# Two linear steps of the VectorE exponential moved to GpSimd, in an attention and MLP block

## Chip, cores, metric

One core of a Trainium2 chip runs the whole program. The metric is the time of one execution on the device, in microseconds (us). Engine names in the profile: PE is TensorE (PEld its weight loads), DVE is VectorE, ACT is ScalarE, POOL is GpSimd, SP is SyncE. The granted clock is the share of TensorE's full clock that the profiler records as granted. PSUM holds the results of TensorE's matmuls; the tiles named `..._sb` lie in SBUF, the on-chip working memory.

A run: "slow" can only mean that it lay more than 1.5% above the fastest run of the same kernel.

## The reference, cut to what matters

```python
def _A_ref(x, wqkv, wo):                      # S = 2048, D = 640, 32 heads of 20
    qkv = (x @ wqkv).reshape(B, S, 3, H, Dh)...
    scores = einsum("bhqd,bhkd->bhqk", q, k) * Dh ** -0.5
    p = softmax(scores)                        # 32 x 2048 x 2048 exponentials
    o = einsum("bhqk,bhkd->bhqd", p, v)
    return o... @ wo
def _B_ref(x, w1, b1, w2, b2):                 # token-mixing MLP, 2048 -> 1536 -> 2048
    ...
xn = layernorm(x)
return x + _A_ref(xn, ...) * silu(_B_ref(xn, ...))
```

The exponentials dominate: 2048 blocks of 128 keys by 512 queries, called units below.

## The kernel before

The program is laid out when it is built. A list scheduler gives every instruction a cost in ns, keeps a clock for each engine, and always places the candidate that can start first. The result is a fixed order for each engine; on the chip an engine runs its order from front to back, and waits on semaphores where data or buffers need it.

```python
def _add(self, eng, ceng, fn, reads, writes, name, extra_req=(), cost=100.0, tail=None):
    ...
    start = self.T[eng]                        # the planner's clock of this engine
    for tt in req.values():                    # what it reads or overwrites
        start = max(start, tt.fin + (self.LAT[eng] if tt.ceng != eng else 0.0))
    ...
    self.T[eng] = start + cost
    t.fin = start + cost + (self.TAIL[eng] if tail is None else tail)
```

ScalarE takes two units in one instruction, from two groups of two PSUM banks. VectorE takes one unit at a time from each of two more banks (4 and 5), by a polynomial on the bits of the score:

```python
ACT_GROUPS = ((0, 1), (2, 3))
DVE_GROUPS = ((4,), (5,))
...
ch = [   # one chain; k is the bank's index
    (lambda e: e.tensor_scalar(w3, lo, 0x7FFF, None, ALU.bitwise_and), bs, [sw], dv(N)),          # PSUM
    (lambda e: e.tensor_scalar(v_, w_, 1.0 / 256.0, -128.0, ALU.mult, ALU.add), [sw], [sv], dv(N, .26)),
    (lambda e: e.tensor_scalar(l_, w_, a3 / 65536.0, (b3 - 64.0 * a3) / 256.0, ALU.mult, ALU.add),
     [sw], [sl_], dv(N, .26)),
    (lambda e: e.tensor_tensor(l_, v_, l_, ALU.mult), [sv, sl_], [sl_], dv(N, .52)),               # product
    (lambda e: e.tensor_tensor(l_, l_, w_, ALU.mult), [sl_, sw], [sl_], dv(N, .52)),               # product
    (lambda e: e.scalar_tensor_tensor(o_, zr, -(self.OFFS - 16256.0), l_, ALU.add, ALU.add),       # PSUM
     bs + [sl_], [S_(f"dpt{s0 + i}") for i in range(n)], dv(N)),
]
```

How many units VectorE gets is decided while the order is laid out: at each refill of a ScalarE group, every VectorE bank that is free by the planner's clock gets a unit in the same batch of score matmuls.

```python
def do_st(grp, us):
    ...
    for dg in self.DVE_GROUPS:
        if dgrp_state[dg] == "free" and len(lst) + len(dg) <= 4 ... and pr.ready("pe", [], [bank_slot[b] for b in dg]) <= T:
            lst += take_dve(dg, rows)
            banks += list(dg)
    emit_st(lst, banks)
```

TensorE's other work (projections, the MLP, products with V) is placed between these batches, along with filler matmuls that the planner adds wherever it counts too few columns in a window, to hold TensorE's granted clock.

The softmax here doesn't subtract the row's maximum and nothing guards it: scores larger than these inputs give would overflow.

Of the kernel before, what the change touches and what calls it, by code (L numbers as in the profile page):

```python
# [7 lines left out]
ALU = mybir.AluOpType  # L8
# [274 lines left out]
class _Kern:  # L283
# [25 lines left out]
    DVE_TAIL_GUARD = 3  # L309
    LAST_GUARD = 10  # L310
    NTMP = 4
    WARM = True
    WARM_MIN = 180.0
    WARM_SLACK = 30.0
# [87 lines left out]
    def schedule(self):  # L402
        pr, t = self.prog, self.t
# [21 lines left out]
        def S_(name):  # L425
            s = sl.get(name)
            if s is None:
                s = sl[name] = _Slot(name)
            return s
# [12 lines left out]
        def dv(n, rate=1.04):  # L442
            return 75.0 + n * rate
# [51 lines left out]
        def small(fn):  # L495
            def f(e):
# [12 lines left out]
                name="id1", cost=300)  # L509
# [5 lines left out]
               cost=200)  # L515
# [8 lines left out]
               writes=[S_("pad")], name="pad", cost=150)  # L524
        pr.dve(lambda e: e.tensor_reduce(cst_sb[:, 1:2], onerow, mybir.AxisListType.X, ALU.add), reads=[S_("idf")],
               writes=[S_("row")], name="pad", cost=130)
        for col, a_, b_, src in ((3, -1.0, 1.0, 0), (4, -CQ0, CQ0, 0), (5, QC, 0.0, 1), (6, KC, 0.0, 1)):
            pr.dve(lambda e, col=col, a_=a_, b_=b_, src=src: e.tensor_scalar(
                cst_sb[:, col:col + 1], cst_sb[:, src:src + 1], a_, b_, ALU.mult, ALU.add),
                reads=[S_("pad"), S_("row")], writes=[S_("cq")], name="cq", cost=90)  # L530
# [535 lines left out]
        dexp = []  # L1066
# [79 lines left out]
        def can_exp():  # L1146
            if not pexp:
                return False
            n = len(pexp[0][0])
            s0 = ptr[0] if ptr[0] + n <= self.RP else 0  # L1150
            return not any(pt_busy[s0:s0 + n])

        dchains = []

        def start_dchain():

            us, banks, grp = dexp[0]
            n = len(us)
            if dptr[0] + n > self.DPT:
                dptr[0] = 0  # L1160
            s0 = dptr[0]
            dexp.pop(0)
            for i in range(n):
                dpt_busy[s0 + i] = True
            dptr[0] = (s0 + n) % self.DPT
            N = n * 512
            zr = ps_all[:, banks[0] * 512:banks[0] * 512 + N]
            lo = zr.bitcast(u16).rearrange("p (n two) -> p n two", two=2)[:, :, 0:1]
            k = self.DVE_GROUPS.index(grp)
            w_, v_, l_ = ew_sb[:, k, 0:N], ev_sb[:, k, 0:N], el_sb[:, k, 0:N]  # L1170
            sw, sv, sl_ = S_(f"ew{k}"), S_(f"ev{k}"), S_(f"el{k}")
            w3 = w_.rearrange("p (n one) -> p n one", one=1)
            o_ = dpt_sb[:, s0:s0 + n, :].rearrange("p a b -> p (a b)").bitcast(u16)
            bs = [bank_slot[b] for b in banks[:n]]
            a3, b3 = self.C3
            ch = [
                (lambda e: e.tensor_scalar(w3, lo, 0x7FFF, None, ALU.bitwise_and), bs, [sw], dv(N)),  # L1177
                (lambda e: e.tensor_scalar(v_, w_, 1.0 / 256.0, -128.0, ALU.mult, ALU.add), [sw], [sv], dv(N, .26)),  # L1178
                (lambda e: e.tensor_scalar(l_, w_, a3 / 65536.0, (b3 - 64.0 * a3) / 256.0, ALU.mult, ALU.add),  # L1179
                 [sw], [sl_], dv(N, .26)),  # L1180
                (lambda e: e.tensor_tensor(l_, v_, l_, ALU.mult), [sv, sl_], [sl_], dv(N, .52)),  # L1181
                (lambda e: e.tensor_tensor(l_, l_, w_, ALU.mult), [sl_, sw], [sl_], dv(N, .52)),  # L1182
                (lambda e: e.scalar_tensor_tensor(o_, zr, -(self.OFFS - 16256.0), l_, ALU.add, ALU.add),  # L1183
                 bs + [sl_], [S_(f"dpt{s0 + i}") for i in range(n)], dv(N)),
            ]
            dchains.append([(x, us, s0, grp) for x in ch])

        def emit_dchain(chn):
            (fn, rd, wr, cost), us, s0, grp = chn.pop(0)
            tk = pr.dve(fn, reads=rd, writes=wr, name=f"dexp{us[0]}", cost=cost)  # L1190
            if not chn:
                dchains.remove(chn)
                dgrp_state[grp] = "free"
                for i, u in enumerate(us):
                    avail.append((tk.fin, u, "d", s0 + i))
# [320 lines left out]
        def pe_cands(T):  # L1516
# [29 lines left out]
            if avail and acc_ok[0]:  # L1546
# [14 lines left out]
                if pick:  # L1561
                    r = max(x[0] for x in pick) + PV_MARGIN
                    pr_ = 1.0 if nav >= self.PV_HI else 30.0 if ramp[0] else (8.0 if pr.gate.warm or not self.WARM else 70.0)
                    c.append((pr_, max(r, pr.ready("pe", [], [sl_acc])), lambda pick=pick: emit_pv(pick)))
            if self.WARM:
                wb = warm_bank()
# [18 lines left out]
            for j in active:  # L1585
                s = j.steps[j.i]
                if s[0] == "pe":
                    c.append((j.prio if pr.gate.warm or not self.WARM else -2.0, pr.ready("pe", s[2], s[3]),
                              lambda j=j: do_step(j, "pe")))
# [60 lines left out]
        def do_step(j, eng):  # L1650
            s = j.steps[j.i]
            j.i += 1
            if s[0] == "ev":
                n = s[8]
                fn = ev_fn(s, eng)
                cost = ac(n) if eng == "act" else dv(n, 0.55 if s[7].startswith("xTe") else 1.04)
                getattr(pr, eng)(fn, reads=s[5], writes=s[6], name=s[7], cost=cost)
            elif s[0] == "pe":
                pe_full(s[1], s[2], s[3], s[4], s[5])
            else:  # L1660
                getattr(pr, s[0])(s[1], reads=s[2], writes=s[3], name=s[4], cost=s[5])
            settle(j)

        def eng_cands(eng, T):
            c = []
            for j in active:
                s = j.steps[j.i]
                if s[0] == eng:
                    c.append((j.prio, pr.ready(eng, s[2], s[3]), lambda j=j: do_step(j, eng)))
                elif s[0] == "ev" and (eng == "dve" or (eng == "act" and (ramp[0]))):  # L1670
                    pen = 0.0 if eng == "dve" else 0.0
                    c.append((j.prio - 30.0 + pen, pr.ready(eng, s[5], s[6]), lambda j=j: do_step(j, eng)))
            if eng == "act" and can_exp():
                us, banks, grp = pexp[0]
                c.append((30.0 if ramp[0] else 48.0, pr.ready("act", [bank_slot[b] for b in banks[:len(us)]], []), emit_exp))
            if eng == "dve":
                for chn in dchains:
                    (fn, rd, wr, cost) = chn[0][0]
                    c.append((90.0 - 0.1 * len(chn), pr.ready("dve", rd, wr), lambda chn=chn: emit_dchain(chn)))
                if dexp and not any(ch[0][3] == dexp[0][2] for ch in dchains):  # L1680
                    us, banks, grp = dexp[0]
                    n = len(us)
                    s0 = dptr[0] if dptr[0] + n <= self.DPT else 0
                    if not any(dpt_busy[s0:s0 + n]):
                        r = pr.ready("dve", [bank_slot[b] for b in banks[:n]], [])

                        def go():
                            start_dchain()
                            emit_dchain(dchains[-1])
                        c.append((90.0, r, go))  # L1690
            return c

        def warm_bank():
            if nxt[0] < 12:
                return AB
            if WB in busybanks or WB in bank_off:
                return None
            return WB
# [18 lines left out]
        while True:  # L1717
# [26 lines left out]
            for e in order:  # L1744
                cs = pe_cands(pr.T[e]) if e == "pe" else eng_cands(e, pr.T[e])
                cs_by[e] = cs

            bt = None
            for e in order:
                if not cs_by[e]:  # L1750
                    continue
                r = min(max(x[1], pr.T[e]) for x in cs_by[e])
# [4 lines left out]
            r, e = bt  # L1757
            if e == "dve" and nxt[0] >= NU:

                soon = [max(x[1], pr.T[e]) for x in cs_by[e] if x[0] <= 12.0]  # L1760
                if soon and min(soon) <= r + 130.0:
                    r = min(soon)
# [45 lines left out]
```

## Time and profile before

| | before |
|---|---|
| time | 869.83 us, median of 2 runs (867.17 to 872.49); 866.5 to 870.8 in the later sessions |
| busy: ScalarE, VectorE, TensorE, GpSimd | 98%, 95%, 92%, 2% |
| units on ScalarE, on VectorE | 1776 (888 instructions), 272 |
| TensorE's granted clock | 1.0 |

A page of the profile lists busy time by engine, then the chain of work that ended last (followed back from the last instruction to what released each step), then groups of equal instructions: count, busy us and mean ns, and the engine's idle time just before them with what ended it. The prediction shows the lines on which it rests.

### The profile page before, as it was taken

What the parts mean: (1) busy time and instruction counts of PE and PEld (TensorE: products, weight loads), DVE (VectorE), ACT (ScalarE), POOL (GpSimd) and SP (SyncE); (2) the same over time, 40 slices, a digit from 0 to 9 for tenths busy, and PEclk for the clock granted to TensorE, in tenths of its full rate; (3) what the DMA queues carried; (4) which work ended last, traced back from release to release, by engine and by line L of the source; (5) the groups of instructions that cost most, each with busy time, mean ns of one, the idle gap of its engine ahead of it and who ended that gap; (6) DMA issues with size and microseconds to landing.
All of it is one profiled execution on the core that took longest, in us unless ns stands there. A gap on an engine that the chain in (4) does not pass through costs nothing.

```text
span 864.8 us, 16498 instructions
## 1 busy us (share of the span) xinstructions
PE 798.6 (92%) x5828; PEld 257.1 (30%) x5918; DVE 823.5 (95%) x2047; ACT 845.3 (98%) x925; POOL 14.0 (2%) x23
## 2 busy tenths in 40 slices
PE   8899999999999999999999999999899998998997
PEld 5422222222222223222322222222222222232233
DVE  8889999999999999999999999999999999999996
ACT  7899999999999999999999999999999999999996
POOL 3200000000000000000000000000000000000000
PEclk9999999999999999999999999999999999999999
DMA  8241010011010313020013022123312201032121
GB/s 236 48 113 30 8 35 10 16 36 31 11 55 15 77 34 89 10 55 10 16 25 78 23 51 52 25 52 71 67 30 46 47 11 11 3 102 69 41 44 35
DMA packets 123350, 39.32 MB, mean 45 GB/s; under 512 B 84312, under 2 KB 122152, under 8 KB 123272
## 3 DMA queue, kind: packets, MB, share of 16 engines
q1 hardware_dynamic: 123272, 38.27, 19.3%
q8 instruction: 50, 0.82, 0.4%
q14 instruction: 28, 0.23, 0.1%
HBM read 25.88 MB, written 9.83 MB: 41 GB/s over the span
## 4 chain that ended last, share of the span: by engine, by line
ACT 87%; PE 10%; DVE 2%; issue 1%; ACTq 0%
ACT pt_sb L1137 85%; PE ps_all L1109 3%; PE ps_all L1224 1%; ACT zt_sb L843 1%; PE ps_all L755 1%; PE ps_all L1702 1%; PE ps_all L879 1%; ACT zt_sb L838 1%; DVE ew_sb L1177 0%; PE ps_all L683 0%; PE ps_all L1710 0%; PE ps_all L722 0%; PE ps_all L703 0%; DVE dpt_sb L1183 0%; DVE el_sb L1181 0%
## 5 line engine op out<-in xcount | busy, mean ns | idle before, releaser
L1137 ACT ACTIVATE pt_sb<-ps_all 128x1024 bf16<-128x1024 f32 x888 | 819.8, 1144 | 3.8 <-PE ps_all L1109 3.0
L1109 PE MATMUL ps_all<-qk_sb 32*128 32x512 bf16 (+1 forms) x2112 | 367.5, 377 | 48.7 <-ACT pt_sb L1137 37.0
L1177 DVE TENSOR_SCALAR ew_sb<-ps_all 128x512 uint16<-128x512 uint16 x272 | 184.2, 685 | 20.7 <-PE ps_all L1109 19.6
L1109 PEld LDWEIGHTS ps_all<-qk_sb 32*128 32x128 bf16 x2112 | 97.3, 91 | 347.2 <-ACT pt_sb L1137 300.7
L1183 DVE SCALAR_TENSOR_TENSOR dpt_sb<-ps_all,el_sb 128x512 uint16<-128x512 f32 x272 | 182.1, 684 | 1.8
L1224 PE MATMUL ps_all<-pt_sb,v_sb 128*32 128x512 bf16 (+1 forms) x1833 | 162.7, 378 | 0.3 <-issue 0.3
L1181 DVE TENSOR_TENSOR el_sb<-ev_sb,el_sb 128x512 bf16<-128x512 bf16 x272 | 111.1, 418 | 1.1
L1182 DVE TENSOR_TENSOR el_sb<-el_sb,ew_sb 128x512 bf16<-128x512 bf16 x272 | 110.3, 418 | 0.9
L1224 PE MATMUL ps_all<-dpt_sb,v_sb 128*32 128x512 bf16 (+1 forms) x279 | 83.7, 379 | 0.0
L810 PE MATMUL ps_all<-regB,regA 128*128 128x128 bf16 (+1 forms) x371 | 75.6, 300 | 2.9 <-issue 1.1
L1178 DVE TENSOR_SCALAR ev_sb<-ew_sb 128x512 bf16<-128x512 uint16 x272 | 75.3, 285 | 2.3
L810 PE MATMUL ps_all<-regC,regA 128*128 128x128 bf16 (+1 forms) x370 | 74.2, 300 | 1.8 <-issue 1.0
L1179 DVE TENSOR_SCALAR el_sb<-ew_sb 128x512 bf16<-128x512 uint16 x272 | 75.1, 284 | 0.0
L722 PE MATMUL ps_all<-xnT_sb,wqk_sb 128*112 128x512 bf16 x200 | 68.2, 405 | 0.4 <-DVE zt_sb L816 0.4
L1224 PEld LDWEIGHTS ps_all<-pt_sb,v_sb 128*32 128x32 bf16 x1833 | 35.4, 94 | 55.5 <-issue 50.4
L1702 PE MATMUL ps_all<-wrm_sb 128*128 128x512 bf16 (+1 forms) x117 | 35.2, 391 | 3.9 <-DVE ps_all L513 2.2
L810 PEld LDWEIGHTS ps_all<-regB,regA 128*128 128x128 bf16 x384 | 25.8, 97 | 39.1 <-issue 23.8
L810 PEld LDWEIGHTS ps_all<-regC,regA 128*128 128x128 bf16 x384 | 25.0, 97 | 39.8 <-issue 28.5
L1710 PE MATMUL ps_all<-wrm_sb,v_sb 128*128 128x512 bf16 x97 | 34.0, 385 | 1.3 <-issue 0.7
L755 PE MATMUL ps_all<-wv_sb,xnT_sb 128*128 128x160 bf16 (+1 forms) x160 | 33.8, 302 | 0.4 <-DVE pk_sb L1030 0.3
L879 PE MATMUL ps_all<-wo_sb,xnT_sb 128*128 128x128 bf16 (+3 forms) x152 | 30.4, 298 | 0.7 <-issue 0.5
L722 PEld LDWEIGHTS ps_all<-xnT_sb,wqk_sb 128*112 128x112 bf16 x200 | 20.7, 127 | 30.6 <-issue 13.4
(89 smaller groups left out, 354.9 us busy)
## 6 DMA issues: line engine op xcount, KB each, us to landing
regA<-in_B_w_dram SPq DMA_DIRECT2D x6, 1024.0 KB
regA<-in_B_w_dram SPq DMA_DIRECT2D x8, 768.0 KB
qkT_scratch_dram<-pk_sb SPq DMA_DIRECT2D x40, 112.0 KB
qk_sb<-qkT_scratch_dram SPq DMA_DIRECT2D x56, 80.0 KB
regA<-in_A_x_dram SPq DMA_DIRECT2D x6, 640.0 KB
on_scratch_dram<-on_sb SPq DMA_DIRECT2D x124, 20.0 KB
out_dram<-regC SPq DMA_DIRECT2D x3, 640.0 KB
wqk_sb<-in_A_wqkv_dram SPq DMA_DIRECT2D x2, 680.0 KB
```

The costliest lines, as they stand in the source:

```text
L722: steps.append(("pe", lambda e, dc=dc: e.matmul(ps_all[0:112, bk * 512:(bk + 1) * 512], wqk_sb[:, dc * 1280 + c0:dc * 1280 + c0 + 112], xn ...
L810: steps.append(("pe", lambda e, k=k: e.matmul(ps(bk, n), wap[:, k, col0:col0 + 128], rows[:, k, c0:c0 + n], start=(k == 0), stop=(k == nk ...
L1109: pr.pe(lambda e, outp=outp, lhsT=lhsT, rhs=rhs, g=g: e.matmul(outp, lhsT, rhs, start=True, stop=True, tile_position=(32 * g, 0)), reads=q ...
L1137: tk = pr.act(lambda e: e.activation(outp, inp, AF.Exp, bias=-self.OFFS * math.log(2.0) / 128.0, scale=math.log(2.0) / 128.0), reads=[bank ...
L1177: (lambda e: e.tensor_scalar(w3, lo, 0x7FFF, None, ALU.bitwise_and), bs, [sw], dv(N)),
L1178: (lambda e: e.tensor_scalar(v_, w_, 1.0 / 256.0, -128.0, ALU.mult, ALU.add), [sw], [sv], dv(N, .26)),
L1179: (lambda e: e.tensor_scalar(l_, w_, a3 / 65536.0, (b3 - 64.0 * a3) / 256.0, ALU.mult, ALU.add), [sw], [sl_], dv(N, .26)),
L1181: (lambda e: e.tensor_tensor(l_, v_, l_, ALU.mult), [sv, sl_], [sl_], dv(N, .52)),
L1182: (lambda e: e.tensor_tensor(l_, l_, w_, ALU.mult), [sl_, sw], [sl_], dv(N, .52)),
L1183: (lambda e: e.scalar_tensor_tensor(o_, zr, -(self.OFFS - 16256.0), l_, ALU.add, ALU.add), bs + [sl_], [S_(f"dpt{s0 + i}") for i in range( ...
L1224: pr.pe(lambda e, outp=outp, lhsT=lhsT, rhs=rhs, k=k, g=g: e.matmul(outp, lhsT, rhs, start=(k == 0), stop=(k == NB - 1), tile_position=(0, ...
L1702: pe_full(lambda e: e.matmul(ps(wb, n), wrm_sb[:, 0:P], wrm_sb[:, P:P + n], start=True, stop=True), [S_("warm"), S_("warm1")], [bank_slot[ ...
```

## The change

The intent is to use the idle GpSimd. VectorE is 95% busy, so two of its six steps, those with one SBUF input and a scalar multiply and add, go to GpSimd; VectorE should then have time for more units, and ScalarE fewer. The first and last steps, which read PSUM, stay on VectorE. The planner gets a cost of 560 ns for a GpSimd step.

```diff
+    POOL_TT = 1150.0
+    POOL_TS = 560.0
 ...
-    (lambda e: e.tensor_scalar(v_, w_, 1.0 / 256.0, -128.0, ALU.mult, ALU.add), [sw], [sv], dv(N, .26)),
+    (lambda e: e.tensor_scalar(v_, w_, 1.0 / 256.0, -128.0, ALU.mult, ALU.add), [sw], [sv], self.POOL_TS, "pool", True),
     (lambda e: e.tensor_scalar(l_, w_, a3 / 65536.0, (b3 - 64.0 * a3) / 256.0, ALU.mult, ALU.add),
-     [sw], [sl_], dv(N, .26)),
+     [sw], [sl_], self.POOL_TS, "pool", True),
 ... (the other four steps gain "dve" as their engine)
     def emit_dchain(chn):
-        (fn, rd, wr, cost), us, s0, grp = chn.pop(0)
-        tk = pr.dve(fn, reads=rd, writes=wr, name=f"dexp{us[0]}", cost=cost)
+        (fn, rd, wr, cost, eng, _), us, s0, grp = chn.pop(0)
+        tk = getattr(pr, eng)(fn, reads=rd, writes=wr, name=f"dexp{us[0]}", cost=cost)
 ... (the chain's next step is offered as a candidate to its own engine)
```

More of the change, by code (lines that the diff above doesn't have):

```diff
@@ L1176, in start_dchain @@
             ch = [
-                (lambda e: e.tensor_scalar(w3, lo, 0x7FFF, None, ALU.bitwise_and), bs, [sw], dv(N)),
-                (lambda e: e.tensor_scalar(v_, w_, 1.0 / 256.0, -128.0, ALU.mult, ALU.add), [sw], [sv], dv(N, .26)),
+                (lambda e: e.tensor_scalar(w3, lo, 0x7FFF, None, ALU.bitwise_and), bs, [sw], dv(N), "dve", False),
+                (lambda e: e.tensor_scalar(v_, w_, 1.0 / 256.0, -128.0, ALU.mult, ALU.add), [sw], [sv], self.POOL_TS, "pool", True),
                 (lambda e: e.tensor_scalar(l_, w_, a3 / 65536.0, (b3 - 64.0 * a3) / 256.0, ALU.mult, ALU.add),
-                 [sw], [sl_], dv(N, .26)),
-                (lambda e: e.tensor_tensor(l_, v_, l_, ALU.mult), [sv, sl_], [sl_], dv(N, .52)),
-                (lambda e: e.tensor_tensor(l_, l_, w_, ALU.mult), [sl_, sw], [sl_], dv(N, .52)),
+                 [sw], [sl_], self.POOL_TS, "pool", True),
+                (lambda e: e.tensor_tensor(l_, v_, l_, ALU.mult), [sv, sl_], [sl_], dv(N, .52), "dve", True),
+                (lambda e: e.tensor_tensor(l_, l_, w_, ALU.mult), [sl_, sw], [sl_], dv(N, .52), "dve", True),
                 (lambda e: e.scalar_tensor_tensor(o_, zr, -(self.OFFS - 16256.0), l_, ALU.add, ALU.add),
-                 bs + [sl_], [S_(f"dpt{s0 + i}") for i in range(n)], dv(N)),
+                 bs + [sl_], [S_(f"dpt{s0 + i}") for i in range(n)], dv(N), "dve", False),
             ]
@@ L1675, in eng_cands @@
                 c.append((30.0 if ramp[0] else 48.0, pr.ready("act", [bank_slot[b] for b in banks[:len(us)]], []), emit_exp))
+            if eng in ("dve", "pool"):
+                for chn in dchains:
+                    (fn, rd, wr, cost, en, _) = chn[0][0]
+                    if en == eng:
+                        r = pr.ready(eng, rd, wr)
+                        c.append((90.0 - 0.1 * len(chn), r, lambda chn=chn: emit_dchain(chn)))
             if eng == "dve":
-                for chn in dchains:
-                    (fn, rd, wr, cost) = chn[0][0]
-                    c.append((90.0 - 0.1 * len(chn), pr.ready("dve", rd, wr), lambda chn=chn: emit_dchain(chn)))
                 if dexp and not any(ch[0][3] == dexp[0][2] for ch in dchains):
```

## The prediction

> **What bounds the kernel now.** I read the page's busy shares first, then its chain that ended last, then the groups by line, then the waits, and last the timeline of two cycles of VectorE.
>
> From the page of the kernel before (busy us, share of the span, instructions; then the chain that ended last):
>
> ```profile
> PE 798.6 (92%) x5828; PEld 257.1 (30%) x5918; DVE 823.5 (95%) x2047; ACT 845.3 (98%) x925; POOL 14.0 (2%) x23
> ...
> ACT 87%; PE 10%; DVE 2%; issue 1%; ACTq 0%
> ```
>
> ScalarE is the bound: 98% busy, and 87% of the chain. VectorE (95%) and TensorE (92%) are close behind; GpSimd is empty. So the change takes work from an engine that is nearly full but is not itself the bound. A gain must come through ScalarE having less to do.
>
> From the groups of the same page (count, then busy us and mean ns of one, then idle before):
>
> ```profile
> L1137 ACT ACTIVATE pt_sb<-ps_all 128x1024 bf16<-128x1024 f32 x888 | 819.8, 1144 | 3.8 <-PE ps_all L1109 3.0
> ...
> L1177 DVE TENSOR_SCALAR ew_sb<-ps_all 128x512 uint16<-128x512 uint16 x272 | 184.2, 685 | 20.7 <-PE ps_all L1109 19.6
> ...
> L1183 DVE SCALAR_TENSOR_TENSOR dpt_sb<-ps_all,el_sb 128x512 uint16<-128x512 f32 x272 | 182.1, 684 | 1.8
> ...
> L1181 DVE TENSOR_TENSOR el_sb<-ev_sb,el_sb 128x512 bf16<-128x512 bf16 x272 | 111.1, 418 | 1.1
> L1182 DVE TENSOR_TENSOR el_sb<-el_sb,ew_sb 128x512 bf16<-128x512 bf16 x272 | 110.3, 418 | 0.9
> ...
> L1178 DVE TENSOR_SCALAR ev_sb<-ew_sb 128x512 bf16<-128x512 uint16 x272 | 75.3, 285 | 2.3
> ...
> L1179 DVE TENSOR_SCALAR el_sb<-ew_sb 128x512 bf16<-128x512 uint16 x272 | 75.1, 284 | 0.0
> ```
>
> A unit is one 128x512 block of exponentials. ScalarE takes two at a time: 888 x 2 = 1776; VectorE takes 272; the sum is 2048. The split is made when the kernel is built: a list scheduler with a cost for each instruction lays out each engine's order, and hands VectorE a unit whenever a VectorE bank is free at a ScalarE refill. The change alters that order everywhere, because two costs and an engine change.
>
> From the waits (total us, times, longest):
>
> ```profile
> PEld ps_all L1109 <- ACT pt_sb L1137: 300.7, 726, 0.9
> ```
>
> TensorE's score matmuls wait for ScalarE's banks. TensorE runs in order, so anything that holds one of its instructions delays ScalarE's next refill, and ScalarE has only two groups of banks, one cadence of cover.
>
> From the timeline of VectorE (start us, us, and count where equal neighbours are merged):
>
> ```profile
> 504.68 1.29 DVE L1177 TENSOR_SCALAR ew_sb<-ps_all 128x512 uint16<-128x512 uint16 x2 [0.41 <-PE ps_all L1109]
> 505.89 0.49 DVE L1178 TENSOR_SCALAR ev_sb<-ew_sb 128x512 bf16<-128x512 uint16 x2
> 506.29 0.49 DVE L1179 TENSOR_SCALAR el_sb<-ew_sb 128x512 bf16<-128x512 uint16 x2
> 506.70 0.42 DVE L1181 TENSOR_TENSOR el_sb<-ev_sb,el_sb 128x512 bf16<-128x512 bf16 x1
> 507.06 0.75 DVE L816 TENSOR_SCALAR zt_sb<-ps_all,b2h_sb 128x512 bf16<-128x512 f32 x1
> 507.73 0.41 DVE L1181 TENSOR_TENSOR el_sb<-ev_sb,el_sb 128x512 bf16<-128x512 bf16 x1
> 508.06 0.75 DVE L1182 TENSOR_TENSOR el_sb<-el_sb,ew_sb 128x512 bf16<-128x512 bf16 x2
> 508.74 1.28 DVE L1183 SCALAR_TENSOR_TENSOR dpt_sb<-ps_all,el_sb 128x512 uint16<-128x512 f32 x2
> 510.18 0.69 DVE L1177 TENSOR_SCALAR ew_sb<-ps_all 128x512 uint16<-128x512 uint16 x1 [0.16 <-PE ps_all L1109]
> ```
>
> Two things are to be seen. Rows overlap: the mean of 285 ns is a latency, and the next one starts 0.20 us later (505.89 to 506.29 for two). Start to start, a step costs 0.60 (PSUM), 0.20 (linear), 0.34 (product). And the two chains of VectorE, one for each of its banks, run almost **in step**: both first steps, both pairs of linear steps, both products, both last steps, with a cycle of 5.5 us.
>
> **What the Trainium skill says.** "SBUF — State Buffer", section "Who interferes with whom": GpSimd has no SBUF port pair of its own, it shares VectorE's second; a VectorE instruction with two SBUF inputs contends with a GpSimd instruction that reads SBUF, and the second to issue "fully blocks" until the first is done. The two products read two SBUF tensors each, so they are exposed; the two PSUM steps have at most one SBUF input and are not. No GpSimd work runs beside these products in the trace before, so it neither confirms nor denies this.
>
> "GPSIMD Engine Reference", section "4.1 Engine selection": one-input elementwise work there is "roughly line-rate". The trace has only memsets to compare: 128x640 at 632 ns and 128x1024 at 957 ns, so 0.85 ns an element and 90 ns fixed. An estimate from these rows for 512 elements is 0.52 us, near the 0.56 us the change assumes; GpSimd's 128x16 TENSOR_SCALAR, though, took 271 ns, so the latency may rather be 0.27 + 496 x 0.85 ns = 0.69 us.
>
> "Perfetto Trace Analysis", section "Optimizing Scalar/DVE Operations": moving work between VectorE and GpSimd "might not help", for the shared port. The trace before cannot test it.
>
> **The change part by part.**
> (1) Removed from VectorE: 2 x 0.20 = 0.40 us a unit, 272 x 0.40 = 109 us (the page's busy sums of 75.3 + 75.1 overstate it). A unit then costs 0.60 + 2 x 0.34 + 0.60 = 1.88 us against 2.28.
> (2) Added to GpSimd: two steps of 0.56 us, 1.12 us a unit; for some 290 units 325 us, under 40% of the span. Its total is no bound.
> (3) What ScalarE could gain: in the timeline 14 activations fill 13.13 us, so about 0.917 us for two units, 0.46 us a unit. VectorE's other work is 823.5 - 272 x 2.28 = 203 us. Were VectorE held only by its sum, it would take about 320 units at the same 95% ((0.95 x 845 - 203) / 1.88 = 319). ScalarE would shed 48 x 0.46 = 22 us: 848 us. That is the ceiling.
> (4) What the latency does to it. Both chains are in step, and both need GpSimd at the same moment. First steps at 0 and 0.6 us; the first chain's linear steps on GpSimd from about 0.8 to 1.95; the second's from 1.95 to 3.1; then its products and last step to about 4.7; then about 0.8 us until the bank is refilled and read. That is 5.5 us, no shorter than now: the 0.40 us gained on VectorE are paid back by 2 x 1.12 us in a row on GpSimd. Before, 136 pairs in about 805 us make a mean cycle of 5.92; if it becomes 5.6, 287 units fit, 15 more, and ScalarE sheds 15 x 0.46 = 7 us. From 870 that is 863 us with no contention.
> (5) Contention. In that picture the first chain's products are due at 2.1 us, just when GpSimd holds the port for the second chain's linear steps. Each meeting costs VectorE 0.3 us (half of one step) to 1.1 us (both steps); I take 0.6 us a cycle. The scheduler knows nothing of it, so the fixed order becomes wrong: VectorE's banks come free late, TensorE stands at the matmul meant for them, and ScalarE's refill stands behind it. Cover is about half a ScalarE cadence, 0.45 us on average, but does not always apply; I let 0.25 us a cycle through. 140 cycles x 0.25 = 35 us. 863 + 35 = 898, which I round to 895.
>
> **The rivals.**
> A: VectorE was holding back the split, the scheduler places the chains out of step, and the port matters little: the ceiling of (3), 846 to 855 us. For it: VectorE's 95%, and GpSimd idle. Against: chains fed by the same matmul batch and two steps in a row on GpSimd.
> B: balance. The longer chain eats the freed time, contention is hidden in VectorE's new slack (5% + 109/865 = 18%, less 3% for 15 more units of 1.88 us: 15%): 860 to 880 us. For it: the slack is real, and a GpSimd wait on a chain leaves VectorE other work.
> C: contention dominates, both linear steps block both products, or GpSimd takes 0.7 us or more with 16-bit integer input: 1 us a cycle let through is 140 us, some 960 us or more; the kernel also places filler matmuls, by its own model of time, to hold TensorE's granted clock (now in the top tenth in all slices), and a stretched order thins them out.
>
> **Range and chances.** My line lies between B and C. 895 us; 848 to 970 should hold it 8 times in 10: the low end is the ceiling, the high end some 0.8 us a cycle let through. Two per cent are 17 us, so faster means under 852: 0.13. Within: 0.30. Slower, above 887: 0.57.
>
> **What would show it.** The count of VectorE units: 285 to 300 for (4), near 320 for A. GpSimd's linear steps spaced 0.5 to 0.6 us for (2). For (5): mean time, or start to start, of the two products well above 418 ns and 0.34 us while the PSUM steps stay at 685 ns; new waits of VectorE for GpSimd; score matmuls waiting for VectorE's last step, now small; ScalarE's idle before its activations, now 3.8 us, grown by tens of us. I am wrong if the products keep their 418 ns, if ScalarE stays at 98%, or if the chains fall out of step.

## The result, and the profile after

The changed kernel took 945.75 us, median of 2 runs (943.54 to 947.96), against 869.83: a ratio of 1.0873 (95% interval 1.0693 to 1.1053). A ratio here and below is the mean time of one kernel's fast runs over that of the other's in the same rounds, so not quite the ratio of the medians quoted.

From the page of the changed kernel (shares, granted clock by slice in tenths, chain that ended last):

```profile
PE 876.1 (93%) x5915; PEld 266.5 (28%) x5915; DVE 785.8 (83%) x1539; ACT 862.3 (91%) x921; POOL 402.7 (43%) x585
...
PEclk9999999999999999799799999759999699589999
...
DVE 46%; PE 23%; POOL 21%; issue 6%; ACT 3%; DMA 1%; DVEq 0%; SPq 0%; ACTq 0%; POOLq 0%
```

ScalarE fell from 98% to 91% of a longer span, and from 87% to 3% of the chain. TensorE is now the busiest, with 93%, but holds only 23% of the chain. The chain runs round a loop: VectorE's first step, two GpSimd steps, products, last step, TensorE's refill. The clock has holes (mean 0.945).

From the groups of the changed kernel:

```profile
L1139 ACT ACTIVATE pt_sb<-ps_all 128x1024 bf16<-128x1024 f32 x884 | 834.3, 1044 | 65.0 <-PE ps_all L1111 59.7
...
L1180 POOL TENSOR_SCALAR ev_sb<-ew_sb 128x512 bf16<-128x512 uint16 x281 | 204.2, 727 | 488.4 <-DVE ew_sb L1179 482.3
...
L1185 DVE SCALAR_TENSOR_TENSOR dpt_sb<-ps_all,el_sb 128x512 uint16<-128x512 f32 x281 | 191.9, 685 | 4.6
...
L1183 DVE TENSOR_TENSOR el_sb<-ev_sb,el_sb 128x512 bf16<-128x512 bf16 x281 | 120.5, 429 | 90.4 <-POOL el_sb L1181 90.0
L1181 POOL TENSOR_SCALAR el_sb<-ew_sb 128x512 bf16<-128x512 uint16 x281 | 184.4, 656 | 17.6
...
L1184 DVE TENSOR_TENSOR el_sb<-el_sb,ew_sb 128x512 bf16<-128x512 bf16 x281 | 139.8, 499 | 5.1
```

VectorE has 281 units, only 9 more, and ScalarE 884 activations, 4 fewer. VectorE waits 90 us for GpSimd before the first product. The second product lasts 499 ns instead of 418; the PSUM step keeps 685. ScalarE's idle before its activations went from 3.8 to 65 us.

From the waits of the kernel before, then of the changed one:

```profile
PEld ps_all L1109 <- DVE dpt_sb L1183: 5.3, 17, 0.4
...
PEld ps_all L1111 <- DVE dpt_sb L1185: 58.6, 118, 1.4
```

This wait grew from 5.3 to 58.6 us: the score matmuls stand at a bank that VectorE's last step has not left, and the refills of ScalarE queue behind.

From the timeline of the changed kernel, first VectorE, then GpSimd, for the same microseconds:

```profile
508.13 1.28 DVE L1179 TENSOR_SCALAR ew_sb<-ps_all 128x512 uint16<-128x512 uint16 x2
510.23 0.42 DVE L1183 TENSOR_TENSOR el_sb<-ev_sb,el_sb 128x512 bf16<-128x512 bf16 x1 [0.82 <-POOL el_sb L1181]
510.69 0.71 DVE L1184 TENSOR_TENSOR el_sb<-el_sb,ew_sb 128x512 bf16<-128x512 bf16 x1
```

```profile
508.90 0.62 POOL L1180 TENSOR_SCALAR ev_sb<-ew_sb 128x512 bf16<-128x512 uint16 x1 [3.60 <-DVE ew_sb L1179]
509.58 0.62 POOL L1181 TENSOR_SCALAR el_sb<-ew_sb 128x512 bf16<-128x512 uint16 x1
510.28 0.86 POOL L1180 TENSOR_SCALAR ev_sb<-ew_sb 128x512 bf16<-128x512 uint16 x1
511.20 0.68 POOL L1181 TENSOR_SCALAR el_sb<-ew_sb 128x512 bf16<-128x512 uint16 x1
```

Two effects can be read here. An undisturbed GpSimd step costs 0.68 to 0.70 us start to start (508.90, 509.58, 510.28), not the planned 0.56. And the first chain's products fall among the second chain's GpSimd steps: the step that begins during a product lasts 0.86 instead of 0.62 us, and the product that begins during that step 0.71 instead of 0.42. In the whole trace 83 second products and 13 first ones (of 281 each) began while a GpSimd step ran, and lasted 0.69 and 0.60 us on average; the rest had 0.42. The stretch shown is not typical in one respect: only 75 of the 280 later chains found GpSimd still busy with the other chain and queued behind it; that is about half of the cycles of two chains.

### The profile page after: what moved, and what is told of

The parts are those of the page before. It is cut to its first block, busy times and chain, and to the rows that moved or that the text cites. A ratio compares the mean times of both kernels' runs of the same rounds, so it can differ in the third digit from the quotient of the medians.

```text
span 945.8 us, 16561 instructions
## 1 busy us (share of the span) xinstructions
PE 876.1 (93%) x5915; PEld 266.5 (28%) x5915; DVE 785.8 (83%) x1539; ACT 862.3 (91%) x921; POOL 402.7 (43%) x585
## 4 chain that ended last, share of the span: by engine, by line
DVE 46%; PE 23%; POOL 21%; issue 6%; ACT 3%; DMA 1%; DVEq 0%; SPq 0%; ACTq 0%; POOLq 0%
POOL ev_sb L1180 10%; DVE ew_sb L1179 10%; POOL el_sb L1181 10%; DVE dpt_sb L1185 9%; DVE el_sb L1183 9%; DVE el_sb L1184 9%; PE ps_all L1111 8%; PE ps_all L1226 4%; PE ps_all L812 3%; ACT pt_sb L1139 2%; DVE zt_sb L818 2%; PE ps_all L724 2%; PE ps_all L1707 1%; PE ps_all L757 1%; DVE on_sb L1287 1%
## 5 line engine op out<-in xcount | busy, mean ns | idle before, releaser
L1139 ACT ACTIVATE pt_sb<-ps_all 128x1024 bf16<-128x1024 f32 x884 | 834.3, 1044 | 65.0 <-PE ps_all L1111 59.7
L1111 PE MATMUL ps_all<-qk_sb 32*128 32x512 bf16 (+1 forms) x2112 | 395.4, 394 | 40.7 <-DVE dpt_sb L1185 22.8
L1180 POOL TENSOR_SCALAR ev_sb<-ew_sb 128x512 bf16<-128x512 uint16 x281 | 204.2, 727 | 488.4 <-DVE ew_sb L1179 482.3
L1185 DVE SCALAR_TENSOR_TENSOR dpt_sb<-ps_all,el_sb 128x512 uint16<-128x512 f32 x281 | 191.9, 685 | 4.6
L1181 POOL TENSOR_SCALAR el_sb<-ew_sb 128x512 bf16<-128x512 uint16 x281 | 184.4, 656 | 17.6
L1226 PE MATMUL ps_all<-pt_sb,v_sb 128*32 128x512 bf16 (+1 forms) x1824 | 175.1, 398 | 0.2 <-DVE tr_sb L1276 0.2
L1184 DVE TENSOR_TENSOR el_sb<-el_sb,ew_sb 128x512 bf16<-128x512 bf16 x281 | 139.8, 499 | 5.1
L1226 PE MATMUL ps_all<-dpt_sb,v_sb 128*32 128x512 bf16 (+1 forms) x288 | 100.9, 400 | 3.0 <-DVE dpt_sb L1185 2.2
L812 PE MATMUL ps_all<-regB,regA 128*128 128x512 bf16 (+1 forms) x384 | 88.3, 325 | 3.4 <-DVE zt_sb L818 1.4
L881 PE MATMUL ps_all<-wo_sb,xnT_sb 128*128 128x512 bf16 (+2 forms) x160 | 34.7, 305 | 1.3 <-DVE regC L895 1.3
L757 PE MATMUL ps_all<-wv_sb,xnT_sb 128*128 128x160 bf16 (+1 forms) x160 | 34.7, 309 | 0.0
```

Of the source, the lines that this page charges most:

```text
L812: steps.append(("pe", lambda e, k=k: e.matmul(ps(bk, n), wap[:, k, col0:col0 + 128], rows[:, k, c0:c0 + n], start=(k == 0), stop=(k == nk ...
L1111: pr.pe(lambda e, outp=outp, lhsT=lhsT, rhs=rhs, g=g: e.matmul(outp, lhsT, rhs, start=True, stop=True, tile_position=(32 * g, 0)), reads=q ...
L1139: tk = pr.act(lambda e: e.activation(outp, inp, AF.Exp, bias=-self.OFFS * math.log(2.0) / 128.0, scale=math.log(2.0) / 128.0), reads=[bank ...
L1226: pr.pe(lambda e, outp=outp, lhsT=lhsT, rhs=rhs, k=k, g=g: e.matmul(outp, lhsT, rhs, start=(k == 0), stop=(k == NB - 1), tile_position=(0, ...
```

## The experiments

Two theories were held against each other. The **latency theory**: a GpSimd step takes 0.12 to 0.14 us more than planned; the order has no room for it, because the two steps of a chain, and where the chains are in step all four, stand one behind the other. The **port theory**: products and GpSimd steps block each other, unplanned. A third, the **order theory**: the new order is bad even when all goes as planned. A fourth question was the granted clock. Where a result is wrong it is said so; the comparison with the reference is too coarse to see such errors, and nothing about accuracy follows from it.

Four runs of each experiment were timed, and seven of the kernel before in each of the three sessions (medians 867.17, 867.52, 866.97). Spacings are start to start, of GpSimd steps that follow each other without a pause; counts of what began during a GpSimd step are from all records of the trace.

### Four runs on the order of after and of before

**e1_tiny.** The order of the changed kernel, identical instruction by instruction on TensorE, VectorE, ScalarE and SyncE; the GpSimd steps work on 16 columns (wrong result).

```diff
-    e.tensor_scalar(v_, w_, 1.0 / 256.0, -128.0, ...)
+    e.tensor_scalar(v_[:, 0:16], w_[:, 0:16], 1.0 / 256.0, -128.0, ...)      # l_ likewise; v_ and l_ zeroed once
```

> The changed kernel in its own order, instruction for instruction, but each GpSimd step works on 16 of the 512 columns (wrong result on purpose). Order theory (the new order is itself bad, both chains meeting at GpSimd): still 910 us or more. Port theory and latency theory (the order is good if GpSimd is as fast as planned and touches no port for long): 855 to 875 us, products back at 418 ns, granted clock 0.99 or more.

Measured: 866.19 us (865.97 to 866.54), ratio 0.9991 (0.9975 to 1.0008). From the page of e1_tiny:

```profile
PE 796.2 (92%) x5826; PEld 257.5 (30%) x5915; DVE 756.7 (88%) x1539; ACT 841.7 (97%) x921; POOL 167.0 (19%) x589
...
ACT 84%; PE 11%; DVE 2%; POOL 1%; issue 1%; ACTq 0%; DVEq 0%; POOLq 0%
```

ScalarE is the bound again. The order theory falls. But the order also gains nothing: VectorE now has slack (88% busy), and the 4 activations saved are worth 4 x 0.917 = 4 us at most. So the whole loss, 77 us by the ratios, comes from what the GpSimd steps do on the chip.

**e2_pow.** The same order; each GpSimd step raises 2 columns of a tile of its own to a power (`ALU.pow`; wrong result). It is as long as a linear step, but reads and writes only these 2 columns.

```diff
-    e.tensor_scalar(v_, w_, 1.0 / 256.0, -128.0, ...)
+    e.tensor_tensor(st_sb[:, 7, 2 * k:2 * k + 2], st_sb[:, 7, 8:10], mhalf(2), ALU.pow)      # waits and releases unchanged
```

> The changed kernel in its own order, but each GpSimd step is a power of 2 columns (697 ns in the trace of before, against 617 to 727 ns of the linear steps), on its own small tile: the latency stays, the port is hardly used (wrong result on purpose). Latency theory (what costs is that a step takes 0.68 us, planned as 0.56): 925 to 950 us. Port theory (what costs is that products and GpSimd steps block each other): 865 to 890 us and products at 418 ns. If a GpSimd instruction holds the port for its whole duration whatever it reads, products stay long and the time too.

Measured: 925.88 us, median of four (912.22 to 939.64). The runs scatter, with granted clocks of 0.94 to 0.98; by the fast two (912.22 and 919.24) the ratio is 1.0561 (1.0514 to 1.0609). The profile fell in a slow run, so only its row durations are used, from the groups of e2_pow:

```profile
L1186 DVE TENSOR_TENSOR el_sb<-ev_sb,el_sb 128x512 bf16<-128x512 bf16 x281 | 118.3, 421 | 102.9 <-POOL st_sb L1184 101.3
L1187 DVE TENSOR_TENSOR el_sb<-el_sb,ew_sb 128x512 bf16<-128x512 bf16 x281 | 117.3, 419 | 5.1
```

The products are back at 420 ns: none of them, not even the 170 that began while a power ran (0.42 us on average), was held. Start to start a power costs 0.67 us (median). So with no product held, about 50 us are lost (1.0561 against 0.9991 of 867), some two thirds of the loss. This is not the latency quite alone: the 112 powers that began during a product lasted 0.82 us instead of 0.70, so products still held GpSimd. As a check on the size: 562 steps x (0.67 - 0.56) = 62 us, if every excess stood on the chain.

**e3_cost690.** The changed kernel (right result), planned with the measured cost.

```diff
-    POOL_TS = 560.0
+    POOL_TS = 690.0
```

> The changed kernel planned with 690 ns for a GpSimd step in place of 560, which is what the trace shows start to start (0.68 to 0.70). Latency theory: the plan fits again, 860 to 885 us. Port theory: the blocking is still unplanned, 910 to 945 us.

Measured: 904.16 us (895.21 to 914.28), ratio 1.0393 (1.0325 to 1.0461). This lies between the two expectations. A truer plan wins back half of the loss, and VectorE's share shrinks to 268 units, fewer than before the change. The products still last 441 and 520 ns here, and the wait of score matmuls for VectorE's last step only falls from 58.6 to 34.7 us. From the waits of e3_cost690:

```profile
PEld ps_all L1111 <- DVE dpt_sb L1185: 34.7, 77, 1.5
```

So something else is still unplanned: 690 ns fits an undisturbed step, but with blocking the mean spacing is 0.76 us.

**e4_dummy.** The kernel before, same order on every engine but GpSimd (right result). After each first step of a chain GpSimd runs two linear steps on scratch tiles, and nobody waits for them.

```diff
+    if len(chn) == 5:                       # the chain's first step was just placed, as tk
+        for i in (0, 1):
+            pr._add("pool", "pool", lambda e, ...: e.tensor_scalar(dmo[:, 2 * k + i, :], dmi, 1.0 / 256.0, -128.0, ALU.mult, ALU.add),
+                    [S_("dmy")], [S_(f"dmo{k}{i}")], ..., extra_req=(tk,), cost=560.0)
```

> The kernel before in its own order and with its right result, VectorE doing all its steps; beside them two GpSimd linear steps of 128x512 on scratch tiles start after each first step of a chain, and nobody waits for them. Port theory: products well above 418 ns (550 or more), linear steps of VectorE too, VectorE being 95% busy the time goes to 900 us or more. Latency theory: nobody waits for GpSimd, so 865 to 875 us.

Measured: 1096.43 us, median of four (1071.82 to 1123.54); only the 1071.82 counts as fast, so there is no interval. The granted clock was 0.77 to 0.83. From the groups of e4_dummy (a slow run; the row durations are VectorE's own, and its first step keeps 681 ns):

```profile
L1182 DVE TENSOR_SCALAR el_sb<-ew_sb 128x512 bf16<-128x512 uint16 x272 | 166.4, 619 | 0.0
L1181 DVE TENSOR_SCALAR ev_sb<-ew_sb 128x512 bf16<-128x512 uint16 x272 | 126.9, 474 | 2.3
L1184 DVE TENSOR_TENSOR el_sb<-ev_sb,el_sb 128x512 bf16<-128x512 bf16 x272 | 114.9, 431 | 1.1
```

Work for which nobody waits costs over 200 us. It is less the products that suffer, as I had expected, than VectorE's linear steps: 474 and 619 ns against 285 and 284. They follow the first step directly and so are the first to come up against GpSimd; 434 of 544 began while it ran, and most of these ended 0.15 us after its step did. Of the 544 products only 28 began while GpSimd ran, and they lasted 0.64 us on average, the others 0.41. The port is real, and its price depends on what of VectorE's work meets GpSimd. How much of the 200 us is the fallen clock's own, no run tells: e6_after_warm below tests the clock only for the changed kernel, at 0.945.

### Four runs that separate the terms

**e10_cols352.** The order of the changed kernel with 352 of 512 columns on GpSimd (wrong result), so that a step takes what was planned: its spacing measured 0.56 us (median; with the steps that products hold, the mean is 0.63), while products still meet it.

```diff
+    e.tensor_scalar(v_[:, 0:352], w_[:, 0:352], 1.0 / 256.0, -128.0, ...)      # l_ likewise
```

> The changed kernel in its own order, GpSimd steps on 352 of 512 columns (wrong result on purpose). From 0.27 us for 16 columns and 0.70 us for 512, start to start, an estimate is 0.56 us, just what was planned; the products still meet them at the port. With the 2-column power (0.67 us, products untouched at 420 ns) the same order took 926 us, with 16 columns 866. Latency theory (the 0.12 us a step above plan costs most): 866 to 885 us. Port theory: 900 us or more, products of 500 ns.

Measured: 873.61 us (871.75 to 880.44), ratio 1.0076 (1.0029 to 1.0124). From the groups of e10_cols352:

```profile
L1186 DVE TENSOR_TENSOR el_sb<-el_sb,ew_sb 128x512 bf16<-128x512 bf16 x281 | 129.5, 462 | 5.1
```

Contention is still there: 108 products began during a GpSimd step and lasted 0.56 us. But where the planned latency holds, it costs 7 us (1.0076 against 0.9991). With e2_pow this gives a table of the one order:

| GpSimd step | median spacing (mean) against plan (0.56) | products blocked | ratio to before |
|---|---|---|---|
| 16 columns (e1_tiny) | 0.27 (0.34), below | none | 0.9991 |
| 352 columns (e10_cols352) | 0.56 (0.63), as planned | yes | 1.0076 |
| power of 2 columns (e2_pow) | 0.67 (0.71), above | none | 1.0561 |
| 512 columns, the change | 0.70 (0.78), above | yes | 1.0873 |

e2_pow stands 5.7% above e1_tiny and e10_cols352 0.9%; the change stands 8.8% above it. The remaining 2.3% (20 us, by the unrounded ratios) would belong to the two effects together. Longer steps block longer (a held product lasted 0.68 us in the changed kernel, 0.56 in e10_cols352), and an order already late has no room to hide it; that reading is argued, not shown. Nor is the remainder sharp: the change's ratio, from two runs, has an interval of 1.8% to each side, and e2_pow's rests on the faster two of four scattered runs.

**x_free.** 16 columns again (wrong result), now planned as 60 ns.

> The ceiling: GpSimd steps on 16 columns (wrong result on purpose) and planned as 60 ns, so VectorE is free of the linear steps and the chain short; VectorE then has 304 units and ScalarE 872 activations (before: 272 and 888). If ScalarE's work sets the time, 16 activations of 0.917 us less: 867 - 15 = 852 us, perhaps 5 us more because a step really takes 0.27 us. If freeing VectorE is worth nothing by itself: 865 or more.

Measured: 886.24 us (876.73 to 900.97), ratio 1.0207 (1.013 to 1.0285); two of the four runs are slow, and the two fast ones (876.73 and 880.89) against the mean of before give only 1.012. It was meant as a ceiling and is not one: its plan errs by 0.2 us a step (0.27 measured, 0.06 planned), the same fault as the change. It shows only that an order with 304 units gains nothing when its steps come late. x_270 below repeats it properly.

**e6_after_warm.** The changed kernel with more filler matmuls (right result).

```diff
-    WARM_OVER = 3600.0; WARM_LAST = 4200.0; WARM_ACC = 3600.0; WARM_FLOOR = 3600.0
+    WARM_OVER = 4400.0; WARM_LAST = 4800.0; WARM_ACC = 4400.0; WARM_FLOOR = 4400.0
```

> The changed kernel with more filler matmuls (targets of 4400 columns a window in place of 3600; 477 fillers against 260), which should hold TensorE's granted clock at 1.0 though the order is stretched. If the slow clock (0.945 in the profile of after) is a large part of the loss: 885 to 915 us at clock 0.99 or more. If the clock is only a consequence: 935 to 960 us, at a better clock.

Measured: 938.29 us (936.22 to 939.82), ratio 1.0805 (1.0779 to 1.0832), at a clock of 0.989. The clock came back, and by the ratios 6 us with it (1.0805 against 1.0873, whose interval is 1.8% to each side): the lowered clock is for the greater part a consequence. The order differs a little (284 units), and more fillers also take TensorE's time, so this is not exact.

**e8_onestep.** Only the second linear step on GpSimd, planned with 690 ns (right result).

```diff
-    ..., [sw], [sv], self.POOL_TS, "pool", True),
+    ..., [sw], [sv], dv(N, .26), "dve", True),
+    POOL_TS = 690.0
```

> Only the second linear step on GpSimd, planned with 690 ns; the first stays on VectorE (right result; 286 units on VectorE, 881 activations). Latency theory: one step fits between, 860 to 875 us. Port theory: half of the meetings remain, and VectorE's own linear step, too, meets GpSimd at the port: 885 to 920 us.

Measured: 885.83 us (882.7 to 889.13), ratio 1.0203 (1.0168 to 1.0238). From the groups of e8_onestep:

```profile
L1180 DVE TENSOR_SCALAR ev_sb<-ew_sb 128x512 bf16<-128x512 uint16 x286 | 115.4, 412 | 2.6
```

The step kept on VectorE lasts 412 ns instead of 285. The 169 instances that began while GpSimd ran averaged 0.50 us (those that were held ended 0.15 us after the GpSimd step), the 117 others 0.29. VectorE is 96% busy: what one step gave it, the other took back. This is the port theory's forecast (885 to 920), at its lower end.

### Four runs on a true plan, and on the port

**x_270.** 16 columns (wrong result), planned as the 270 ns that they take undisturbed (median 0.27 us, mean 0.35, in its trace).

> The ceiling again, now planned truthfully: GpSimd steps on 16 columns (wrong result on purpose), planned as 270 ns, which is their measured spacing. VectorE has 299 units, ScalarE 875 activations, 13 fewer than before. If a true plan and a free VectorE are worth their activations: 867 - 13 x 0.917 = 855 us, 850 to 862. If the freed VectorE time is worth nothing even then: 865 or more, like the 866 of 16 columns planned as 560.

Measured: 857.69 us (857.35 to 857.88), ratio 0.9893 (0.9876 to 0.9909). From the page of x_270:

```profile
PE 788.8 (92%) x5822; PEld 256.9 (30%) x5908; DVE 784.8 (92%) x1611; ACT 834.2 (97%) x912; POOL 185.6 (22%) x625
...
ACT 80%; PE 13%; DVE 3%; POOL 2%; issue 2%; ACTq 0%; DVEq 0%; POOLq 0%
```

The idea is sound, but small: VectorE takes 299 units, ScalarE's 13 fewer activations are worth 13 x 0.917 = 12 us, and 9 are measured. This is what a GpSimd step of 0.27 us that holds no product would bring; with 512 columns the step measured 0.70 us.

**e11_full_cost.** The changed kernel (right result), planned with what its trace shows under contention: the mean spacing of back-to-back GpSimd steps was 0.78 us.

```diff
-    POOL_TS = 560.0
+    POOL_TS = 780.0
-    ..., [sv, sl_], [sl_], dv(N, .52), "dve", True),          # both products
+    ..., [sv, sl_], [sl_], dv(N, .52) + 40.0, "dve", True),
```

> The changed kernel (right result) planned with what its trace shows under contention: 780 ns for a GpSimd step, 40 ns more for a product. VectorE has 255 units, ScalarE 897 activations, 9 more than before. If the loss is the plan's error: 867 + 9 x 0.917 = 875 us, 868 to 888, clearly under the 904 of the plan with 690. If the blocking costs whatever the plan says: 895 us or more. Neither theory sees it faster than before.

Measured: 880.37 us (879.87 to 880.83), ratio 1.0155 (1.014 to 1.017). From the page of e11_full_cost:

```profile
PE 808.8 (92%) x5847; PEld 260.8 (30%) x5936; DVE 740.3 (84%) x1435; ACT 855.0 (97%) x934; POOL 362.2 (41%) x533
...
ACT 78%; PE 14%; DVE 4%; POOL 1%; issue 1%; DMA 1%; ACTq 0%; POOLq 0%; DVEq 0%
```

GpSimd's steps are all but off the chain (1%), ScalarE is back on it (78%), and the clock is 1.0. The products still last 435 and 508 ns, but the plan allows for it. So blocking that is planned for is affordable; the plan's error was not. What remains against before is work: the chains are so long now that VectorE gets only 255 units, and 9 more activations take 9 x 0.917 = 8 us of the 13.

**e9_onechain.** One chain uses GpSimd (planned 690 ns), the other stays on VectorE (right result).

```diff
-    ..., [sw], [sv], self.POOL_TS, "pool", True),             # and l_ likewise
+    ..., [sw], [sv], self.POOL_TS if k else dv(N, .26), "pool" if k else "dve", True),
+    POOL_TS = 690.0
```

> Only one of the two chains uses GpSimd for its two linear steps (planned 690 ns), the other stays wholly on VectorE (right result; 276 units, 886 activations). If the loss comes from both chains queueing at GpSimd: 865 to 878 us. If it comes from blocking at the port (the other chain's own linear steps are exposed too): 885 to 910 us.

Measured: 888.46 us (885.67 to 892.01), ratio 1.0251 (1.0216 to 1.0285). From the groups of e9_onechain (the VectorE half):

```profile
L1181 DVE TENSOR_SCALAR el_sb<-ew_sb 128x512 bf16<-128x512 uint16 x151 | 54.4, 360 | 0.0
L1180 DVE TENSOR_SCALAR ev_sb<-ew_sb 128x512 bf16<-128x512 uint16 x151 | 47.5, 314 | 2.0
```

With no queue of two chains at GpSimd, the time still stays over 2% above before. The linear steps left on VectorE are lengthened (314 and 360 ns), the products too (439 and 454). That speaks for the port in this variant. How much of the 22 us is blocking and how much an imperfect plan, this run does not tell.

**e5_dummyw.** As e4_dummy, but GpSimd only writes: a memset of 512 columns in place of each linear step (right result).

> As the kernel before with idle GpSimd work beside it that nobody waits for, but memsets of 512 columns in place of linear steps: GpSimd only writes. If a product is blocked only by a GpSimd instruction that reads, products stay at 418 ns; VectorE's linear steps, if they hold the write port too, stay long (450 to 620 ns); the time lies between 867 and the 1096 of the reading kind, say 950 to 1060. If writing blocks nothing: 867 to 875.

Measured: 1084.77 us, median of four (1069.23 to 1101.39); by the fast two, ratio 1.2362 (1.2329 to 1.2396), a little above the expected range. From the groups of e5_dummyw (a slow run, read as in e4_dummy):

```profile
L1181 DVE TENSOR_SCALAR ev_sb<-ew_sb 128x512 bf16<-128x512 uint16 x272 | 156.3, 582 | 2.3
L1182 DVE TENSOR_SCALAR el_sb<-ew_sb 128x512 bf16<-128x512 uint16 x272 | 138.7, 517 | 0.0
L1184 DVE TENSOR_TENSOR el_sb<-ev_sb,el_sb 128x512 bf16<-128x512 bf16 x272 | 109.5, 411 | 1.1
```

Writing alone holds VectorE's linear steps as badly as reading does. The products have 411 ns. Whether a product that begins beside a GpSimd memset is held is not tested and stays open: none of the 544 products began while one ran. The other way round the trace tells something, as far as GpSimd's records can be trusted: 82 memsets began during a product, and neither was longer for it (0.52 us, the median of the others too; the products 0.41), while the 82 reading steps of e4_dummy that began during a product had a median of 0.73 us against 0.65.

No experiment with a right result beats the kernel before, so there is no better version to run.

## Why the prediction was right or wrong, point by point

The verdict (slower, most likely) was right, and 945.75 us lies inside 848 to 970, but 51 us above the predicted 895. It reached its direction with a term missing, the steps' excess over the plan; that the number came as near as it did is in part luck.

- **What bounds it, and where a gain must come from**: right. e1_tiny and x_270 bring ScalarE back to the chain, and x_270 gains roughly what its 13 activations are worth.
- **Step (2), GpSimd's cost**: this is the step that failed. It took "two steps of 0.56 us" and called GpSimd's total no bound. The total is none (43% busy), but the spacing is 0.70 us. The prediction had noted that 0.69 us was possible, and did not carry that into the sum: it used 0.56 in step (4) and left 0.7 us to rival C. The missing term is 562 steps x 0.14 us = 79 us at most; e2_pow, with 0.67, measures about 50, GpSimd's waits for products included.
- **Step (4), the chain's length**: right in direction, though its picture holds in only about half of the cycles. "In step" was read from one stretch of 6 us: in the whole trace before, 79 first steps follow the other chain's within 1.3 us, of at most 136 such pairs; in the changed kernel 74 of 140, and 75 chains queue at GpSimd. VectorE gained only 9 units. The forecast was 15, worth 7 us from 870, so 863; the order alone, with quick GpSimd steps, gave 866, which is no gain on 867.
- **Step (5), contention**: seen; its size stays open. The products lengthened as foretold, VectorE waited for GpSimd, score matmuls waited for VectorE's last step (5.3 to 58.6 us), ScalarE's idle before its activations grew from 3.8 to 65 us. The prediction charged 35 us to contention alone. e10_cols352 shows 7 us where latency is as planned, but its shorter steps block less; e3_cost690, planned with the undisturbed latency, still loses 34 us by its ratio, in an order of its own. So 35 us may have been about right: no run has the full blocking, and nothing else, in the order of the change.
- **The unplanned delay gets through to ScalarE**: right, and the most general part. Much the same GpSimd work (562, 536 and 510 steps) costs, by the ratios to before, 76 us in an order planned with 560 ns, 34 with 690, and 13 with 780, where 8 of the 13 are work given back to ScalarE.
- **Rival A** failed: the ceiling was put at 848 us by VectorE's sum, with 320 units. With a short, truly planned step it is 858 and 299 units, and with a real step it is never reached. **Rival C** was right about 0.7 us, and about the clock (0.945); e6_after_warm speaks against the clock as the main cause. Its number does not follow from its sum: 140 us on 863 are 1003, not "some 960".
- **One sum**: 13.13 us for 14 activations are 0.94 us each, not 0.917; the trace's median spacing is 0.90, so nothing hangs on it.

## What to carry to other kernels

In a program whose order is fixed in advance, an instruction moved to another engine must be planned with its start-to-start spacing beside the work that it will meet: 0.14 us of error in each of 562 steps of one loop cost about 50 us, where the move, with short and truly planned steps, gained 9. Before moving work off an engine that is full but not the bound, work out what the bound sheds; here it was 4 activations, 4 us, against two steps of each chain that now take 0.70 us where they took 0.20. Work moved from VectorE to GpSimd can lengthen what stays: moving one of two linear steps here lengthened the other from 285 to 412 ns.

## What the Trainium skill lacked or had wrong

- "SBUF — State Buffer", section "SBUF: two separate sides", says that whoever starts first holds the shared pair for the whole instruction. A GpSimd power of 2 columns that ran 0.7 us held no product: the 170 that began during one lasted 0.42 us on average, while the 96 that began during a 512-column linear step lasted 0.68. So the time shown for a GpSimd instruction is not the time for which it holds the pair; that its access to SBUF decides is inferred.
- The same page, section "Who interferes with whom", is borne out where VectorE's linear steps meet GpSimd (285 to 474 and 619 ns against reading, 582 and 517 against writing; most that were held ended 0.15 us after the GpSimd step), but gives no price in a fixed order: GpSimd work that nobody waited for took this kernel from 867 to 1072 us and more, at a granted clock of 0.83 and less.
- "GPSIMD Engine Reference", section "4.1 Engine selection", calls one-input work "roughly line-rate" and the page gives no fixed cost of one GpSimd instruction. A multiply-add from 16-bit integers to bf16 was spaced 0.27, 0.56 and 0.70 us for 16, 352 and 512 columns, which is 0.26 us and 0.87 ns a column; the same step of 512 columns on VectorE was spaced 0.20 us, so here GpSimd was 3.5 times slower.
- No page read gives the delay of a handover from VectorE to GpSimd and back: in the timeline of after, the GpSimd step starts 0.77 us after the start of a first step that is itself spaced 0.60 us, and the product 0.03 us after the GpSimd step's end. Over the whole trace the medians are 0.08 us from the end of the first step's record to the GpSimd step, and 0.03 us back.
